# Moving the first weight sums of an MLP behind a different residual addition, at the edge between attention and MLP

## The chip, the cores and the metric

The kernel runs on one core of one Trainium2 chip. The metric is the device time of the whole program in microseconds (us). It is quoted as a median over runs. Where two kernels are compared, the ratio is the mean time of one kernel's fast runs over the mean time of the other's fast runs of the same rounds on the same chip, with a 95% interval. It is therefore not quite the ratio of the medians that stand beside it.

Engines carry the names of the profile: PE is TensorE's matmul unit, DVE is VectorE, ACT is ScalarE, POOL is GpSimd, and SPq is the queue of SyncE, which issues most DMAs. "L560" is line 560 of the kernel. The edits of the experiments shift later lines by up to 18: L640 of the kernel before is L642 or L644 in some runs, L729 is L731, L828 is up to L846.

## The reference

One transformer layer on x of 2048 x 1024 in bf16: linear attention with 32 heads of 32, then a gated MLP with 3584 hidden columns. Each stands behind a layer norm and is added to its input.

```python
def attention(x, wqkv, wo):                 # x: 2048 x 1024, already normalised
    q, k, v = heads(x @ wqkv)               # 32 heads of 32
    phi = lambda t: jnp.where(t > 0, t + 1, jnp.exp(t)) + 1e-6
    pq, pk = phi(q), phi(k)
    kv, z = pk^T @ v, sum(pk)               # per head
    num, den = pq @ kv, pq @ z + 1e-6
    return merge(num / den) @ wo

def mlp(x, W_gate, W_up, W_down):           # x already normalised
    return (relu(x @ W_gate) * (x @ W_up)) @ W_down

h  = x + attention(layernorm(x), wqkv, wo)
h2 = h + mlp(layernorm(h), W_gate, W_up, W_down)
```

## The kernel before

Everything is fused in one program. The large products are computed with a seven-product scheme instead of eight (as Strassen's). A block of four outputs, called a quad here, is computed by the products m1 to m7. These need sums of the left blocks (of the normalised x, `hn`) and sums of the right blocks (of the weights), and VectorE makes both. In the profile, the PSUM tile `Aq` holds m1, then m6, m7 and m4 on top of it, `Dq` holds m2, and `Eq` m5 and then m3. ScalarE copies some of these tiles to SBUF between the products (L154); the copies are called snapshots here.

The change touches one stretch, about 205 to 290 us: the **edge** between attention and the MLP. Rows come in tiles of 128, tile 0 to 15 in the order of work. The first eight tiles give the first half, on which the first MLP quads ("early quads") can start while attention still works on the second half. For each tile the attention stages are these:

- `nd` makes numerators and denominators (PE), then the reciprocal (ACT) and the division (DVE).
- `oT` is a transpose by DMA.
- `wo_h` is the product with wo (PE) and the x addition in two halves (DVE). The addition also frees the PSUM bank that the product stood in. Mean and norm (DVE, ACT) follow.
- `hn_T` is the DMA transpose of the normalised tile, four steps after `nd`; `wo_h` comes two steps after `nd`. For tiles 4 to 7 (and 12 to 15 of the second half), four left sums follow on DVE.

```python
    def left_sums(T, S, cols, eng):                                      # for tiles 4 to 7 of a half
        ...
        eng.tensor_tensor(out=s1, in0=a21, in1=a22, op=ALU.add)          # L117
        eng.tensor_tensor(out=s2, in0=s1, in1=a11, op=ALU.subtract)      # L118
        eng.tensor_tensor(out=a21.bitcast(FP16), in0=a11, in1=a21, op=ALU.subtract)
        eng.tensor_tensor(out=s4, in0=a12, in1=s2, op=ALU.subtract)      # L120

    def phi_end(dst, e):
        nc.scalar.activation(out=e, in_=dst, func=ACT.Exp, bias=negb[:, 0:1], scale=1.0)   # L216
        nc.vector.tensor_scalar(out=e, in0=e, scalar1=1.0, scalar2=PHI_EPS, op0=ALU.min, op1=ALU.add)
        nc.vector.tensor_tensor(out=dst, in0=dst, in1=e, op=ALU.max)                       # L218

        def wo_h(borrow):                                                # of attn_stages(t)
            ...
            for j in range(2):
                ...                                                      # a PSUM bank, ps
                for c in range(KC):
                    nc.tensor.matmul(ps[:], lhsT=st["oT"][:, c, :], rhs=wo_sb[...], ...)   # L557
                with tc.high_priority():
                    added[t] = nc.vector.scalar_tensor_tensor(           # L560, the x addition
                        out=h_sb[...], in0=ps[:], scalar=1.0, in1=h_sb[...],
                        op0=ALU.mult, op1=ALU.add, accum_out=tot[:, j:j + 1])

    def weight_sums(w_sb, fi, nm):                                       # four per weight and quad
        ...
        steps = [first,                                                  # L636
            lambda: tt(out=t[0][:, 1], in0=b[1][1], in1=t[0][:, 0], op=ALU.subtract),   # L640
            lambda: tt(out=t[0][:, 2], in0=b[1][1], in1=b[0][1], op=ALU.subtract),      # L641
            lambda: tt(out=t[0][:, 3], in0=b[1][0], in1=t[0][:, 1], op=ALU.subtract)]   # L642

    # the first early quad begins without its sums; they come later:
    for step in range(QSTEPS + 2, ready):
        if step == QSTEPS + 2:
            flow.pop(0)()
        attn_step(step)
    with tc.issue_after(added[order[STS - 1]].ins):                      # L779, STS = 8
        late_sums.pop()()                                                # 4 gate and 4 up sums
```

A scheduler orders the instructions of each engine in this part. `issue_after` adds one constraint to it: what stands inside is issued behind the instruction named. `added[t]` is overwritten by the second half, so `added[order[7]]` is the last x addition of tile 7.

Of the kernel before, what the change touches and what calls it, by code (L numbers as in the profile page):

```python
# [31 lines left out]
def block_kernel(ctx: ExitStack, tc: tile.TileContext, x, wqkv, wo, wg, wu, wd, out, H: int):  # L32
    nc = tc.nc
# [10 lines left out]
    NW = 512  # L44
# [176 lines left out]
    order = [(i * HS + s * SW) // P + tt for s in range(NS) for i in range(2) for tt in range(NT)]  # L221
# [289 lines left out]
    held, added, squared = [], {}, {}  # L511

    def attn_stages(t):

        i, r = divmod(t * P, HS)
        s, r = divmod(r, SW)
        st = {}

        def nd():
            o_sb = bwork.tile([P, D], BF16, tag="o_sb", name="o_sb")  # L520
            st["o"] = o_sb
            held.append(o_sb)
            ov = o_sb[:].rearrange("p (k h e) -> p k h e", k=KC, h=HPC)
            for c0, n in pieces:
                ps = ndpool.tile([P, NW], FP32, tag="ab", name="nd")
                for c in range(c0, c0 + n):
                    nc.tensor.matmul(ps[:, (c - c0) * NDW:(c - c0 + 1) * NDW], lhsT=pqT[:, c, t * P:(t + 1) * P],
                                     rhs=kvz[:, c, :], start=True, stop=True)
                ndv = ps[:, 0:n * NDW].rearrange("p (k w) -> p k w", w=NDW)
                den = bsmall.tile([P, GPB, HPC], FP32, tag="den", name="den")  # L530
                nc.scalar.activation(out=den[:, 0:n], in_=ndv[:, :, P:NDW], func=ACT.Ln, bias=deps[:], scale=1.0)
                rd = bsmall.tile([P, GPB, HPC], FP32, tag="rd", name="rd")
                nc.scalar.activation(out=rd[:, 0:n], in_=den[:, 0:n], func=ACT.Exp, scale=-1.0)  # L533
                nc.vector.tensor_tensor(  # L534
                    out=ov[:, c0:c0 + n], in0=ndv[:, :, 0:P].rearrange("p k (h e) -> p k h e", h=HPC),
                    in1=rd[:, 0:n, :].unsqueeze(3).to_broadcast([P, n, HPC, Dh]), op=ALU.mult)

        def oT():
            oT = bwork.tile([P, D], BF16, tag="oT", bufs=XB, name="oT")
            st["oT"] = oT[:].rearrange("p (c t) -> p c t", c=KC)  # L540
            nc.sync.dma_start_transpose(out=st["oT"], in_=st["o"][:])

        def x_in():
            x_sb = bwork.tile([P, D], BF16, tag="x_res", bufs=XB, name="x_res")
            nc.sync.dma_start(out=x_sb[:], in_=xf[t * P:(t + 1) * P, :])
            st["x"] = x_sb

        def wo_h(borrow):
            h_sb = st["x"]
            tot = bsmall.tile([P, 2], FP32, tag="tot", name="tot")  # L550
            for j in range(2):
                if borrow:
                    ps = pspool.tile([P, NW], FP32, tag="E", bufs=2, name="attn")
                else:
                    ps = abpool.tile([P, NW], FP32, tag="ab", name="attn")
                for c in range(KC):
                    nc.tensor.matmul(ps[:], lhsT=st["oT"][:, c, :], rhs=wo_sb[:, c, j * NW:(j + 1) * NW],  # L557
                                     start=(c == 0), stop=(c == KC - 1))
                with tc.high_priority():
                    added[t] = nc.vector.scalar_tensor_tensor(out=h_sb[:, j * NW:(j + 1) * NW], in0=ps[:], scalar=1.0,  # L560
                                                   in1=h_sb[:, j * NW:(j + 1) * NW], op0=ALU.mult, op1=ALU.add,
                                                   accum_out=tot[:, j:j + 1])
            nc.sync.dma_start(out=h_dram[i][s][:, r // P, :], in_=h_sb[:])
            st["hn"] = bwork.tile([P, D], BF16, tag="hn", bufs=HB, name="hn")

            sm = bsmall.tile([P, 6], FP32, tag="sm", name="sm")
            nmean, var, lnv, rstd, nmr = (sm[:, i:i + 1] for i in range(5))
            nc.vector.tensor_scalar(out=nmean, in0=tot[:, 0:1], scalar1=tot[:, 1:2], scalar2=-1.0 / D,
                                    op0=ALU.add, op1=ALU.mult)
            squared[t] = nc.scalar.activation(out=st["hn"][:], in_=h_sb[:], func=ACT.Square, bias=nmean, scale=1.0, accum_out=var)  # L570
            nc.scalar.activation(out=lnv, in_=var, func=ACT.Ln, bias=LN_EPS, scale=1.0 / D)
            nc.scalar.activation(out=rstd, in_=lnv, func=ACT.Exp, scale=-0.5)
            nc.scalar.activation(out=nmr, in_=nmean, func=ACT.Identity, scale=rstd)
            nc.scalar.activation(out=st["hn"][:], in_=h_sb[:], func=ACT.Identity, bias=nmr, scale=rstd)

        def hn_T():
            nc.sync.dma_start_transpose(out=hnT[s][i][:, :, r:r + P], in_=st["hn"][:])

        return nd, oT, x_in, wo_h, hn_T

    LAG = (0, 1, 1, 2, 4)
    STS = ST // NS
# [4 lines left out]
    def attn_step(step):  # L587
        for k in range(len(LAG)):
            n = step - LAG[k]
            if n in begin_at:  # L590
                n = begin_at.index(n)
                if k == 3:
                    stages[n][k](QSTEPS <= step < STS + LAG[-1])
                else:
                    stages[n][k]()
                if k == len(LAG) - 1 and n % STS >= NT:
                    left_sums(hnT[n // STS], hns[n // STS], slice(n % NT * P, (n % NT + 1) * P), nc.vector)
# [177 lines left out]
    for step in range(QSTEPS + 2, ready):  # L775
        if step == QSTEPS + 2:
            flow.pop(0)()
        attn_step(step)
    with tc.issue_after(added[order[STS - 1]].ins):  # L779
        late_sums.pop()()  # L780
    steps = QSTEPS + STS + LAG[-1] - ready
    for n in range(steps):
# [19 lines left out]
    def acc(tag):  # L802
        return accs.tile([P, 2 * NW], FP32, tag=tag, bufs=2 if tag == "A" else 1, name="acc" + tag)
# [119 lines left out]
    for r, (wt, f, fi, toks) in enumerate(runs):  # L923
        w = [ops() for _, ops in now]
        later = []
        for n, s in enumerate(toks):
# [51 lines left out]
            if k == nwin - 3:  # L978
                for x in range(2):
                    t = wpools[1].tile([P, KC * 2 * GP * P], BF16, tag=("wg", "wu")[x], name="wd")  # L980
# [16 lines left out]
    for n in range(2):  # L997
        t = fpool.tile([P, 4 * D], BF16, tag="wraw", bufs=2, name="xd")
# [244 lines left out]
    for n in range(1, len(OUTER)):  # L1243
# [73 lines left out]
        else:  # L1317
            pss = []
            for p in range(4):
                ps = acc(("A", "A", "XY"[(n + 1) % 2], "XY"[n % 2])[p])  # L1320
# [24 lines left out]
@with_exitstack  # L1345
def kernel(
    ctx: ExitStack,
    tc: tile.TileContext,
    A_x: bass.AP,
    A_wqkv: bass.AP,  # L1350
    A_wo: bass.AP,
    B_x: bass.AP,
    B_W_gate: bass.AP,
    B_W_up: bass.AP,
    B_W_down: bass.AP,
    out: bass.AP,
):
    block_kernel(tc, A_x, A_wqkv, A_wo, B_W_gate, B_W_up, B_W_down, out, H=32)
# [30 lines left out]
```

## Time and profile before

Three runs gave a median of 738.58 us (737.89 to 739.36).

| stretch before | value | read from |
|---|---|---|
| span of the profiled run | 737.3 us | head of the page |
| PE busy | 724.7 us (98%) | busy time |
| DVE busy in 210 to 220 us | 9.89 of 10 us | windows |
| PE busy in 210 to 220 us | 8.19 of 10 us | windows |
| PE's recorded waits in 203 to 292 us | 2.0 us | waits |
| first matmul of the main quads | 287.84 us | PE's timeline |

The page of the kernel before gives busy time, share of the span and number of instructions by engine. Further down it gives the shares of the chain that ended last:

```profile
PE 724.7 (98%) x4020; PEld 382.1 (52%) x4020; DVE 563.8 (76%) x992; ACT 322.4 (44%) x580; POOL 5.6 (1%) x44
...
PE 82%; DVE 8%; DMA 5%; ACT 4%; issue 1%; SPq 0%; DVEq 0%; POOL 0%; ACTq 0%
```

As a whole the kernel is bound by TensorE. The edge is not. The windows view of the kernel before has the columns stretch, length, busy time and count of PE, PEld, DVE, ACT and POOL, the granted TensorE clock, the DMA share and GB/s:

```profile
210.00:220.00 10.00, 8.19 (x49) 4.02 (x48) 9.89 (x30) 8.55 (x28) 0.00 (x0) 1.00 0.69 129
220.00:230.00 10.00, 9.90 (x53) 4.62 (x51) 8.66 (x23) 7.47 (x22) 0.00 (x0) 1.00 0.96 204
```

In the first of these stretches DVE is full and PE is not. The Trainium skill (Perfetto Trace Analysis, section "Optimization Strategy") says that the most contended engine can change from one regime of a kernel to the next, and that one should look for the gaps of the engine within the regime and for the instruction that ends each. PE's waits in 203 to 292 us of the kernel before are these (who waited for whom: total us, times, longest us):

```profile
PE attn L557 <- DVE x_res L560: 1.3, 1, 1.3
PE nd L527 <- DVE o_sb L534: 0.5, 1, 0.5
PE attn L557 <- DVE o_sb L534: 0.2, 1, 0.2
```

In PE's timeline of the kernel before (start us, length us, engine, line, operation, out<-in, form, count, and in brackets the idle time before and who ended it) the largest is the wo product of tile 9, which waits for tile 8's addition to free a bank:

```profile
207.78 3.61 PE L557 MATMUL attn<-wo_mem,oT 128*128 128x512 bf16 x16
212.73 0.59 PE L557 MATMUL attn<-wo_mem,oT 128*128 128x512 bf16 x2 [1.34 <-DVE x_res L560]
...
219.20 1.03 PE L729 MATMUL Aq<-hs,tg 128*128 128x512 f16 x4
```

DVE's timeline of the kernel before shows what stood ahead of that addition (same columns). The five lines at L636 to L642 are sums of the first quad's weights, `tg` of the gate and `tu` of the up weight. L217 is phi's min and add, L560 the addition. The lines left out are left sums:

```profile
208.63 0.42 DVE L636 TENSOR_TENSOR tg<-wg 128x512 f16<-128x512 bf16 x1
208.97 0.42 DVE L641 TENSOR_TENSOR tg<-wg 128x512 f16<-128x512 bf16 x1
...
209.64 0.42 DVE L640 TENSOR_TENSOR tg<-wg,tg 128x512 f16<-128x512 bf16 x1
...
210.98 0.42 DVE L642 TENSOR_TENSOR tg<-wg,tg 128x512 f16<-128x512 bf16 x1
211.32 0.42 DVE L636 TENSOR_TENSOR tu<-wu 128x512 f16<-128x512 bf16 x1
211.65 0.42 DVE L217 TENSOR_SCALAR e<-e 128x1024 bf16<-128x1024 bf16 x1
211.99 0.68 DVE L560 SCALAR_TENSOR_TENSOR x_res<-attn,x_res 128x512 bf16<-128x512 f32 x1
```

The min/add at L217 needs the exp of ScalarE. ScalarE's timeline of the kernel before has it at:

```profile
209.94 1.14 ACT L216 ACTIVATE e<-pq_mem,negb 128x1024 bf16<-128x1024 bf16 x1
```

Before the change the exp is not what the addition waits for. It ends at 211.08, and VectorE is still at its sums until 211.65.

### The profile page before, as it was taken

What the parts mean: (1) busy time and instruction counts of PE and PEld (TensorE: products, weight loads), DVE (VectorE), ACT (ScalarE), POOL (GpSimd) and SP (SyncE); (2) the same over time, 40 slices, a digit from 0 to 9 for tenths busy, and PEclk for the clock granted to TensorE, in tenths of its full rate; (3) what the DMA queues carried; (4) which work ended last, traced back from release to release, by engine and by line L of the source; (5) the groups of instructions that cost most, each with busy time, mean ns of one, the idle gap of its engine ahead of it and who ended that gap; (6) DMA issues with size and microseconds to landing.
All of it is one profiled execution on the core that took longest, in us unless ns stands there. A gap on an engine that the chain in (4) does not pass through costs nothing.

```text
span 737.3 us, 10605 instructions
## 1 busy us (share of the span) xinstructions
PE 724.7 (98%) x4020; PEld 382.1 (52%) x4020; DVE 563.8 (76%) x992; ACT 322.4 (44%) x580; POOL 5.6 (1%) x44
## 2 busy tenths in 40 slices
PE   7999999999999999999999999999999999999997
PEld 3444555444444444444444444444444468888666
DVE  6997644677788777688768787887786379996797
ACT  4876553778887654444344444443444120000000
POOL 1000000000000000000000000000000000000000
PEclk9999999999999999999999999999999999999999
DMA  9765002079977526175638358575483499987822
GB/s 315 159 151 159 1 1 85 31 159 222 221 172 179 128 73 207 43 207 136 196 103 243 114 187 272 185 218 195 158 284 116 140 396 335 333 288 296 295 81 78
DMA packets 146594, 132.02 MB, mean 179 GB/s; under 512 B 50928, under 2 KB 128112, under 8 KB 146544
## 3 DMA queue, kind: packets, MB, share of 16 engines
q1 hardware_dynamic: 135536, 123.30, 55.8%
q10 hardware_dynamic: 11008, 8.06, 3.4%
q8 instruction: 31, 0.51, 0.3%
q14 instruction: 19, 0.16, 0.1%
HBM read 79.95 MB, written 39.85 MB: 162 GB/s over the span
## 4 chain that ended last, share of the span: by engine, by line
PE 82%; DVE 8%; DMA 5%; ACT 4%; issue 1%; SPq 0%; DVEq 0%; POOL 0%; ACTq 0%
PE accA L828 22%; PE accY L828 8%; PE accX L828 8%; PE accA L1160 8%; PE attn L557 5%; PE Aq L314 3%; PE accA L989 3%; PE accX L1160 3%; PE Aq L454 3%; PE accY L1160 2%; PE Aq L729 2%; PE Eq L314 2%; PE accY L989 2%; PE accX L989 2%; PE Eq L454 1%; PE Eq L729 1%
## 5 line engine op out<-in xcount | busy, mean ns | idle before, releaser
L838 ACT ACTIVATE gu<-gu 128x512 bf16<-128x512 bf16 x72 | 45.4, 630 | 131.2 <-DVE gu L837 131.2
L833 ACT COPY snap<-accA 128x1024 f32<-128x1024 f32 x72 | 72.5, 1008 | 36.5 <-PE accA L828 36.4
L557 PE MATMUL attn<-wo_mem,oT 128*128 128x512 bf16 x256 | 58.7, 379 | 2.7 <-DVE x_res L560 1.3
L828 PEld LDWEIGHTS <-tu 128*128 128x128 f16 x384 | 37.6, 98 | 45.3
L828 PEld LDWEIGHTS <-tg 128*128 128x128 f16 x384 | 37.6, 98 | 45.3
L837 DVE TENSOR_TENSOR gu<-accY,snap 128x1024 bf16<-128x1024 f32 x36 | 43.9, 1219 | 10.0 <-ACT snap L833 10.0
L828 PE MATMUL accA<-hn,tg 128*128 128x512 f16 (+1 forms) x192 | 49.3, 379 | 0.0
L828 PE MATMUL accA<-hn,tu 128*128 128x512 f16 (+1 forms) x192 | 49.3, 379 | 0.0
L837 DVE TENSOR_TENSOR gu<-accX,snap 128x1024 bf16<-128x1024 f32 x36 | 43.9, 1219 | 6.4 <-PE accX L828 3.7
L154 ACT COPY u<-Aq 128x512 f32<-128x512 f32 x54 | 31.3, 582 | 36.0 <-PE Aq L314 19.3
L1160 PEld LDWEIGHTS <-x 128*128 128x128 f16 (+1 forms) x448 | 43.9, 98 | 5.5
L828 PEld LDWEIGHTS <-wu 128*128 128x128 bf16 x288 | 28.2, 98 | 34.0
L828 PEld LDWEIGHTS <-wg 128*128 128x128 bf16 x288 | 28.2, 98 | 34.0
L557 PEld LDWEIGHTS <-oT 128*128 128x128 bf16 x256 | 24.7, 98 | 33.0 <-issue 4.9
L841 DVE TENSOR_TENSOR hq<-gu 128x512 bf16<-128x512 bf16 x48 | 20.3, 423 | 14.3 <-ACT gu L838 14.2
L314 PEld LDWEIGHTS <-xT 128*128 128x128 bf16 (+1 forms) x192 | 18.6, 98 | 23.7 <-issue 2.3
L534 DVE TENSOR_TENSOR o_sb<-nd,rd 128x384 bf16<-128x384 f32 (+1 forms) x48 | 23.2, 508 | 8.8 <-ACT rd L533 6.6
L1160 PEld LDWEIGHTS <-xs 128*128 128x128 f16 x280 | 27.4, 98 | 3.2
L560 DVE SCALAR_TENSOR_TENSOR x_res<-attn,x_res 128x512 bf16<-128x512 f32 x32 | 22.0, 686 | 8.4 <-PE attn L557 8.2
L989 PEld LDWEIGHTS <-x 128*128 128x128 bf16 (+1 forms) x168 | 16.4, 98 | 19.6
L1166 DVE TENSOR_TENSOR snap<-accA,u 128x1024 f32<-128x1024 f32 x16 | 19.5, 1220 | 8.3 <-PE accA L1160 8.1
L828 PE MATMUL accA<-hs,tg 128*128 128x512 f16 x96 | 24.6, 379 | 0.0
(234 smaller groups left out, 1406.1 us busy)
## 6 DMA issues: line engine op xcount, KB each, us to landing
x<-x_dram SPq DMA_DIRECT2D x17, 896.0 KB, 8.3
x_dram<-hq SPq DMA_DIRECT2D x28, 512.0 KB, 3.2
wg<-in_B_W_gate_dram SPq DMA_DIRECT2D x14, 512.0 KB, 5.2
wu<-in_B_W_up_dram SPq DMA_DIRECT2D x14, 512.0 KB, 7.3
wraw<-in_B_W_down_dram SPq DMA_DIRECT2D x14, 512.0 KB, 5.0
x_dram<-hq SPq DMA_DIRECT2D x28, 256.0 KB, 2.6
t_dram<-wt SPq DMA_DIRECT2D x28, 256.0 KB, 2.2
xd<-x_dram SPq DMA_DIRECT2D x6, 896.0 KB, 7.2
```

What stands on the lines that cost most here:

```text
L154: copies[nm, v] = nc.scalar.copy(out=snaps[nm, v], in_=bank[v][:])
L314: nc.tensor.matmul(ps[:], lhsT=left[m - 1][:, kc, r + v * P:r + (v + 1) * P], rhs=right[m - 1][:, kc, :], start=(start and kc == 0), stop= ...
L454: nc.tensor.matmul(ps[:], lhsT=rq[m - 1][:, kc, (c + v) * P:(c + v + 1) * P], rhs=left[m - 1][:, kc, :], start=(start and kc == 0), stop=( ...
L534: nc.vector.tensor_tensor(out=ov[:, c0:c0 + n], in0=ndv[:, :, 0:P].rearrange("p k (h e) -> p k h e", h=HPC), in1=rd[:, 0:n, :].unsqueeze(3 ...
L557: nc.tensor.matmul(ps[:], lhsT=st["oT"][:, c, :], rhs=wo_sb[:, c, j * NW:(j + 1) * NW], start=(c == 0), stop=(c == KC - 1))
L729: nc.tensor.matmul(ps[:], lhsT=w(v, m)[:, kc, :], rhs=left[m - 1][:, kc, :], start=(start and kc == 0), stop=(kc == KH - 1), skip_group_ch ...
L828: nc.tensor.matmul(ps[:, v, :], lhsT=w[v][n - 1][:, kc, :], rhs=left[n - 1][:, kc, :], start=(t is not None and kc == 0), stop=(kc == KH - ...
L833: nc.scalar.copy(out=st[nm][:], in_=halves(st["A"]))
L837: add(out=g[:], in0=halves(st[nm]), in1=st[base][:], op=ALU.add)
L838: nc.scalar.activation(out=g[:, 0, :], in_=g[:, 0, :], func=ACT.Relu)
L989: nc.tensor.matmul(ps[:, t * NW:(t + 1) * NW], lhsT=x_tile(n, s, kh)[:, f, (t0 + t) * P:(t0 + t + 1) * P], rhs=w_tile(n, kh)[:, f, :], sta ...
L1160: nc.tensor.matmul(pv[:, tt, :], lhsT=left(m)[:, f, tt * P:(tt + 1) * P], rhs=right(m)[:, f, :], start=(t is not None and f == 0 and tt % ...
```

## The change

Its intent is to take the first quad's weight sums out of the way of tile 8's first x addition. The constraint names tile 8's first addition instead of tile 7's last.

```diff
-                    added[t] = nc.vector.scalar_tensor_tensor(out=h_sb[:, j * NW:(j + 1) * NW], ...
+                    added[t, j] = nc.vector.scalar_tensor_tensor(out=h_sb[:, j * NW:(j + 1) * NW], ...
@@
-    with tc.issue_after(added[order[STS - 1]].ins):
+    with tc.issue_after(added[order[STS], 0].ins):
         late_sums.pop()()
```

The number of instructions is the same. A comparison of the two built programs' instruction orders (it has no times) shows that all five sums leave the place in front of tile 8's first addition. One sum stands ahead of tile 9's first addition, where another stood before. Seven follow the left sums made after that, where two stood. PE's order follows: in the first quad four gate matmuls of m5 instead of two come first and m5 of the up weight comes earlier, and in the second quad seven m6 matmuls now stand ahead of tile 12's wo matmuls.

More of the change, by code (lines that the diff above doesn't have):

```diff
@@ L559, in wo_h @@
                 with tc.high_priority():
-                    added[t] = nc.vector.scalar_tensor_tensor(out=h_sb[:, j * NW:(j + 1) * NW], in0=ps[:], scalar=1.0,
+                    added[t, j] = nc.vector.scalar_tensor_tensor(out=h_sb[:, j * NW:(j + 1) * NW], in0=ps[:], scalar=1.0,
                                                    in1=h_sb[:, j * NW:(j + 1) * NW], op0=ALU.mult, op1=ALU.add,
```

## The prediction

> **What bounds the kernel.** TensorE. The page gives it 724.7 us busy of a 737.3 us span at full clock; the chain of waits is 82% PE. The change touches only the edge between attention and the early MLP quads, about 205 to 290 us. The stretch view (10 us slices, 200 to 290) shows PE idle there for about 2.3 us, 1.8 of it in 210 to 220: no reordering here can win more (0.3%).
>
> **The gap.** PE waits twice: 1.34 us at 212.73 (wo matmuls of tile 9) for the first x addition of tile 8 (211.99, 0.68 us), which frees their PSUM bank, then 0.48 us at 213.80 (numerators) for the division behind it. In VectorE's timeline five weight sums stand ahead of that addition, 208.63 to 211.65, 0.335 us apart: 1.67 us. The Trainium skill (PSUM — Partial Sum Buffer, "Engine vs sequencer instructions") says that VectorE's and ScalarE's queues are strict FIFO; the trace agrees: the addition's matmuls had ended near 209.6.
>
> **What the change does.** Nothing is added or removed. The comparison of instruction orders shows all five sums leaving that place; one sum of the first quad stays ahead of tile 9's first addition (where another stood), seven follow tile 9's left sums, where two stood. PE's order follows: four instead of two m5 gate matmuls first, m5 of the up weight earlier, and in the second quad seven m6 matmuls ahead of tile 12's wo matmuls.
>
> **Worth on the critical path.**
> - Not 1.67 us. Before the addition stands phi's min/add on VectorE (211.65), which needs ScalarE's exp, 209.94 to 211.08, in an unchanged ScalarE order. So the min/add starts near 211.13, the addition near 211.47, PE near 212.2: gain 0.52 us. The 0.48 us gap moves along and stays.
> - Given back: tile 9's left sums end near 219.2, the first quad's m6 gate sum near 219.6, while PE, after Dq x4 and Eq x4 (8 x 0.216 us), is ready at 219.1: a new stall of 0.4 to 0.5 us. The up weight's first sum ends near 220.65, PE ready at 220.5: another 0.1 to 0.2.
> - VectorE's backlog is then 1.1 us larger, until its idle time at 227 to 230 absorbs it.
> - Weight matmuls ahead of later wo groups may close the gaps at 228.8, 239.2 and 249.0 (0.09, 0.10, 0.24 us): up to 0.4 gained. m7 directly before m4 may cost 0.1 to 0.3 waiting for ScalarE's snapshots.
>
> Sum: -0.5 +0.6 -0.4 +0.15, about -0.2 us; from 290 us on nothing changes. These are estimates from the trace's starts and durations.
>
> **Prediction:** 738.4 us, 80% range 737.3 to 739.6 (runs of before: 737.9 to 739.4). Faster by over 2%: 0.005; within 2%: 0.985; slower by over 2%: 0.01.
>
> **What the profile should show.**
> 1. Tile 8's first addition starts 0.5 us earlier (not 1.7), directly behind the min/add that waits for the exp.
> 2. PE's 1.34 us wait shrinks to about 0.8; the 0.5 us one for the division stays.
> 3. A new PE wait on a weight sum, 0.3 to 0.7 us near 219.5.
> 4. PE's idle time from 200 to 290 within 1 us of 2.3; the first main quad (287.84 before) starts within 1 us of that.
> 5. Equal instruction counts; PE busy equal within 0.5 us.
>
> **What would make it wrong.** A late buffer release or DMA transpose (the queue's order of oT and hn changes), stalling 1 to 3 us in the second or third quad; a larger sum stall because tile 9's transposed tile lands later; or, the other way, hidden sums and closed gaps, a gain of 1 to 2 us.

One name in it is wrong. The "left sums of tile 9" and "tile 9's transposed tile" are those of tile 7: in the first half left sums are made for tiles 4 to 7 only, and they come two steps later than the wo product. The times given there are of the right instructions.

## The result

The changed kernel took 739.2 us (median of 6 runs, 739.13 to 739.61). The kernel before took 738.94 us beside it (6 runs, 737.88 to 740.4). The ratio is 1.0005, with a 95% interval of 0.9992 to 1.0018: the same time. The changed kernel was correct, and its profiled run ended at full clock, with a span of 737.3 us, equal to the one before.

The page of the changed kernel:

```profile
PE 722.0 (98%) x3967; PEld 381.7 (52%) x4020; DVE 563.8 (76%) x992; ACT 321.6 (44%) x580; POOL 5.6 (1%) x44
...
PE 84%; DVE 6%; DMA 5%; ACT 4%; issue 1%; SPq 0%; DVEq 0%; POOL 0%; ACTq 0%
```

PE's 722.0 is not a gain of 2.7 us. The trace lacks 53 matmul records (3967 against 4020), while the weight loads, which match the matmuls one for one before, are 4020 in both. A second trace of the changed kernel (`e6_after_again`), with all 4020 records, has 725.5 us. DVE's busy time is equal to the digit. The windows of the changed kernel:

```profile
210.00:220.00 10.00, 8.26 (x48) 3.83 (x47) 9.02 (x26) 9.07 (x33) 0.00 (x0) 1.00 0.78 151
220.00:230.00 10.00, 9.92 (x50) 4.37 (x50) 9.46 (x26) 6.23 (x17) 0.00 (x0) 1.00 0.70 179
```

VectorE's work went from the first stretch (9.89 to 9.02 us) to the second (8.66 to 9.46 us). The sum of both is 18.55 us before and 18.48 us after. PE gained nothing that could be seen: 18.09 and 18.18 us, the second with records missing.

PE's waits of the changed kernel in 203 to 292 us:

```profile
PE attn L557 <- DVE x_res L560: 0.8, 1, 0.8
PE nd L527 <- DVE o_sb L534: 0.5, 1, 0.5
PE Aq L729 <- DVE tg L640: 0.4, 1, 0.4
PE attn L557 <- DVE o_sb L534: 0.4, 1, 0.4
```

This is the whole result in small. The list adds up to 2.1 us, against 2.0 us before. The half microsecond that left the first line has come back in the third and fourth. PE's timeline of the changed kernel shows where:

```profile
207.44 3.61 PE L557 MATMUL attn<-wo_mem,oT 128*128 128x512 bf16 x15
211.86 0.59 PE L557 MATMUL attn<-wo_mem,oT 128*128 128x512 bf16 x2 [0.81 <-DVE x_res L560]
...
219.53 1.04 PE L729 MATMUL Aq<-hs,tg 128*128 128x512 f16 x4 [0.45 <-DVE tg L640]
...
249.84 3.61 PE L557 MATMUL attn<-wo_mem,oT 128*128 128x512 bf16 x15 [0.40 <-DVE o_sb L534]
```

In DVE's timeline of the changed kernel the five sums are gone from the place ahead of the addition. Only 0.53 us of their 1.67 us are won, because the min/add now stands idle for 0.94 us, waiting for the exp. At 219 the sums are late in turn, directly behind the last left sums:

```profile
210.78 0.43 DVE L217 TENSOR_SCALAR e<-e 128x1024 bf16<-128x1024 bf16 x1 [0.94 <-ACT e L216]
211.12 0.69 DVE L560 SCALAR_TENSOR_TENSOR x_res<-attn,x_res 128x512 bf16<-128x512 f32 x1
...
218.72 0.42 DVE L120 TENSOR_TENSOR hs<-hn,hs 128x512 f16<-128x512 bf16 x1
219.06 0.42 DVE L640 TENSOR_TENSOR tg<-wg,tg 128x512 f16<-128x512 bf16 x1
```

The exp itself, in ScalarE's timeline of the changed kernel, starts 0.34 us earlier, as much as PE's wo product of tile 8 (207.44 against 207.78):

```profile
209.60 1.14 ACT L216 ACTIVATE e<-pq_mem,negb 128x1024 bf16<-128x1024 bf16 x1
```

The addition therefore starts 1.52 us after the exp's start, where before it started 2.05 us after it.

The chain of work that ended last says the same in another way (start us, length us, what). In this stretch of the kernel before it ran through the weight sums:

```profile
209.06 0.34 DVE tg L641
...
211.32 0.42 DVE tu L636
211.74 0.34 DVE e L217
212.07 0.07 DVE x_res L560
```

In the changed kernel it no longer does. It runs through ScalarE's exp and norm, then a DMA transpose of tile 7, its left sums, and only then a weight sum:

```profile
209.71 1.04 ACT e L216
...
211.28 1.17 ACT hn L574
...
212.86 4.70 DMA hn<-hn
...
217.58 0.43 DVE hs L117
...
219.14 0.35 DVE tg L640
```

One chain was shortened. Another, nearly as long, took its place.

### The profile page after: what moved, and what is told of

It reads as the page before. It is cut to its first block, busy times and chain, and to the rows that moved or that the text cites. A ratio compares the mean times of both kernels' runs of the same rounds, so it can differ in the third digit from the quotient of the medians.

```text
span 737.3 us, 10550 instructions
## 1 busy us (share of the span) xinstructions
PE 722.0 (98%) x3967; PEld 381.7 (52%) x4020; DVE 563.8 (76%) x992; ACT 321.6 (44%) x580; POOL 5.6 (1%) x44
## 4 chain that ended last, share of the span: by engine, by line
PE 84%; DVE 6%; DMA 5%; ACT 4%; issue 1%; SPq 0%; DVEq 0%; POOL 0%; ACTq 0%
PE accA L828 22%; PE accX L828 8%; PE accY L828 8%; PE accA L1160 8%; PE attn L557 6%; PE Aq L314 3%; PE Aq L729 3%; PE accA L989 3%; PE accX L1160 3%; PE Aq L454 3%; PE accY L1160 2%; PE Eq L314 2%; PE accY L989 2%; PE accX L989 2%; PE Eq L729 2%
## 5 line engine op out<-in xcount | busy, mean ns | idle before, releaser
L828 PEld LDWEIGHTS <-tu 128*128 128x128 f16 x384 | 37.6, 98 | 45.3
L828 PEld LDWEIGHTS <-tg 128*128 128x128 f16 x384 | 37.6, 98 | 45.3
L828 PE MATMUL accA<-hn,tu 128*128 128x512 f16 (+1 forms) x192 | 49.3, 379 | 0.0
L828 PE MATMUL accA<-hn,tg 128*128 128x512 f16 (+1 forms) x192 | 49.3, 379 | 0.0
L828 PEld LDWEIGHTS <-wu 128*128 128x128 bf16 x288 | 28.2, 98 | 34.0
L828 PEld LDWEIGHTS <-wg 128*128 128x128 bf16 x288 | 28.2, 98 | 34.0
L828 PE MATMUL accA<-hs,tg 128*128 128x512 f16 x96 | 24.6, 379 | 0.0
```

Of the source, the lines that this page charges most:

```text
L828: nc.tensor.matmul(ps[:, v, :], lhsT=w[v][n - 1][:, kc, :], rhs=left[n - 1][:, kc, :], start=(t is not None and kc == 0), stop=(kc == KH - ...
```

## The experiments

**The theory of two chains** is that of the prediction, extended by what the traces showed. The edge is paced by VectorE and ScalarE together. Taking the sums away wins only what is left above the exp, and the sums come back later, in front of PE, because VectorE's total work is unchanged. **The rival of PE's order**: the gain was won, and PE's new order (seven m6 matmuls ahead of tile 12's wo) gave it back. **The inert rival**: nothing at the edge matters, because TensorE's volume sets its end. The expectations quoted below were written before each run and use the names and the knowledge of that moment.

The runs were sent in three jobs. The kernel before ran in each: median 739.0 us in the first (11 runs, 738.48 to 741.2), 739.05 in the second (11 runs), 739.38 in the third (11 runs). Most main differences are below 1 us, so a ruler better than the total time was needed. Two facts made one.

- From the first main quad on, the length hardly differs. The span minus the start of that quad is 449.45 to 449.55 us in eleven of the twelve traces (449.1 in `e4_sums_on_pool`).
- The launches differ before the edge. PE reaches the first early quad anywhere between 204.6 and 207.3 us. The Trainium skill (TensorE: Matmul & The Clock Gate, section "What's actually happening") says that the clock is throttled by default, that activity releases it, and that an idle window of about 3.4 us brings it back to half. The traces agree in the main. Near the start PE waits once for VectorE (`tp<-ident,xn`, at 9 to 10 us). This wait was 3.71, 3.02 and 3.24 us in `e5_before_again`, `e6_after_again` and `e8_both_phi_second`; the granted clock then fell to 0.50 until 14 to 15 us, and PE reached the edge at 206.5 to 207.3. In the other nine traces it was 1.63 to 2.63 us, the clock in 10 to 20 us was 1.00, and PE reached the edge at 204.6 to 205.5.

The ruler used below is therefore the time **from the start of the last exp (L216) to the first main-quad matmul (L828)**. Why it starts at the exp and not at PE is told at the repeats. The expectations still use the length from tile 8's first wo matmul to the main quads. It came out at 80.06 and 79.51 us (before, e5), 80.38 and 79.42 (after, e6), 79.66 (e1), 79.76 (e2), 79.21 and 78.51 (e3, e9), 79.63 (e8), 81.66 (e7) and 86.12 (e4). So e1 and e3 lie inside what the theory of two chains expected, and e5, e6, e7 and e8 outside.

| trace | last exp | tile 8's first addition | first main matmul | exp to main | ratio of times [95%] |
|---|---|---|---|---|---|
| before | 209.94 | 211.99 | 287.84 | 77.90 | |
| e5_before_again | 211.06 | 213.11 | 289.00 | 77.94 | 1.0007 [0.9991, 1.0023] |
| after | 209.60 | 211.12 | 287.82 | 78.22 | 1.0005 [0.9992, 1.0018] |
| e6_after_again | 210.06 | 211.58 | 288.09 | 78.03 | 0.9998 [0.9982, 1.0013] |
| e1_two_early | 208.73 | 210.25 | 286.95 | 78.22 | 0.9986 [0.9973, 0.9999] |
| e2_phi_late | 209.13 | 209.29 | 286.75 | 77.62 | 0.9991 [0.9975, 1.0006] |
| e3_both | 209.99 | 210.69 | 287.04 | 77.05 | 0.9982 [0.9969, 0.9995] |
| e9_both_again | 208.62 | 209.33 | 285.71 | 77.09 | 0.9986 [0.9968, 1.0003] |
| e8_both_phi_second | 211.42 | 212.12 | 288.89 | 77.47 | 0.9981 [0.9966, 0.9996] |
| e7_m6_behind | 209.45 | 210.96 | 288.94 | 79.49 | 1.0016 [1.0002, 1.0031] |
| e4_sums_on_pool | 209.92 | 216.67 | 293.88 | 83.96 | 1.0072 [1.0057, 1.0087] |
| e10_rd_first | 205.94 (moved) | 210.06 | 290.38 | not comparable, see e10 | 1.0035 [1.0016, 1.0054] |

All outputs were correct.

### Two sums early, so that PE does not wait for them at 219 (e1)

The sums that the first m6 and m5 products need are put back where VectorE has 0.94 us of idle time; the rest stay behind tile 8's addition. The second quad's sums are held behind tile 9's second addition, so that the scheduler cannot fill the freed place with them.

```diff
+            if f == 1:
+                with tc.issue_after(added[order[STS + 1], 1].ins):
+                    sums()
+            elif f:
                 sums()
@@
+    gate, up = all_sums(early[0], 0)
+    with tc.issue_after(added[order[STS - 1], 1].ins):
+        for f in gate[0][:2]:
+            f()
     with tc.issue_after(added[order[STS], 0].ins):
-        late_sums.pop()()
+        for f in gate[0][2:] + up[0]:
+            f()
```

> After the change, with two of the eight sums (the gate's first and second) put back ahead of tile 8's first x addition, and the second quad's sums held behind tile 9's additions so that they cannot fill the place. Edge length = from tile 8's first wo matmul to the first main-quad matmul: before 80.06 us, after 80.38. Queue theory (VectorE's order decides, and 0.94 us of it was idle behind the exp): the addition stays as early as after the change (about 3.7 us behind the start of tile 8's wo matmuls; before it was 4.2), the 0.45 us wait for the second gate sum goes, edge length 79.5 to 79.9. Rival (the edge's idle time is not what sets the time, later waits take it up): wait gone but edge length 80.0 to 80.4. Time of the whole kernel within 0.3% of before either way.

Measured: 738.57 us (738.23 to 738.72, 5 runs). The addition again starts 1.52 us after the exp, and PE's wait for a weight sum is gone. In its place stands, in PE's timeline of this kernel, a wait for tile 7's left sum:

```profile
217.71 0.59 PE L729 MATMUL Eq<-hs,tg 128*128 128x512 f16 x2 [0.51 <-DVE hs L117]
```

In DVE's timeline of the same kernel, that left sum waits for the DMA transpose:

```profile
217.23 0.43 DVE L117 TENSOR_TENSOR hs<-hn 128x512 f16<-128x512 bf16 x1 [0.62 <-DMA hn<-hn]
```

It follows that the weight sums were not alone at 219. The chain exp, norm, transpose, left sum stands right behind them. With the sums out of the way PE waits for the transpose about as long as it had waited for the sum (0.51 against 0.45 us), and exp to main stays 78.22 us. That length is not this wait's alone: the scheduler also changed PE's order further on (tile 12's wo matmuls start at 237.39 us, ahead of m2 and m6).

### Phi's min/add and max behind the addition (e2)

This takes away what caps the gain: the addition need not wait for the exp if phi's last two VectorE steps stand behind it.

```diff
-        nc.vector.tensor_scalar(out=e, in0=e, scalar1=1.0, scalar2=PHI_EPS, op0=ALU.min, op1=ALU.add)
-        nc.vector.tensor_tensor(out=dst, in0=dst, in1=e, op=ALU.max)
+        a = nc.vector.tensor_scalar(...)                       # unchanged
+        phi_end.last = a, nc.vector.tensor_tensor(...)         # unchanged
@@ tile 7's left sums, held where they were
+                    ctx7 = tc.issue_after(added[order[STS + 1], 1].ins) if n == STS - 1 else ExitStack()
@@ behind the late sums
+    for i in phi_end.last:                                     # an order on VectorE, no data
+        tc.add_manual_dep(i.ins, added[order[STS], 0].ins.name, ...)
```

> After the change, with the last phi's min/add and max on VectorE put behind tile 8's first x addition (tile 7's left sums held behind tile 9's additions). If the exp is what capped the gain: the addition starts 2.3 to 2.6 us behind the start of tile 8's wo matmuls instead of 3.7, tile 9's wo matmuls no longer wait (0.81 us after the change), the wait for the division stays near 0.45. VectorE cannot pass the exp by more than the one addition, so edge length falls by 0.3 to 0.5 only, to about 80.0 us; the 0.45 us wait for the second gate sum stays. Rival (the addition is bound by something else): start stays at 3.5 to 3.7.

Measured: 738.57 us (737.71 to 740.56, 6 runs). The addition starts 0.16 us after the exp's start, 2.30 us after the wo matmuls', as expected, and PE's wait for it is gone. This settles what capped the gain of the change: it was the exp. The expectation missed on the next wait. The division's wait was to stay at about 0.45 us; it is 0.85 us, in PE's timeline of this kernel:

```profile
211.45 0.33 PE L527 MATMUL nd<-kvz,pq_mem 128*128 128x132 bf16 x3 [0.85 <-DVE o_sb L534]
```

Two waits that had stood one behind the other have become one. Of the 1.3 us of both in the changed kernel (0.81 and 0.48), 0.4 us is saved. The wait for a weight sum, 0.45 us, stays.

### Both edits (e3, and again as e9)

> Both of these edits together. Queue theory: the addition 2.9 to 3.2 us behind the start of the wo matmuls, tile 9's wo matmuls wait under 0.2, no wait for a weight sum, edge length 79.1 to 79.6; the kernel about 0.7 to 1.0 us faster than after (0.1%), not to be resolved by times alone. Rival of a downstream that takes it up: 80.0 or more.

Measured: 738.37 us (737.69 to 738.5, 5 runs). Exp to main is 77.05 us, 0.9 us less than before and 1.1 us less than after (means of the two traces each, 77.92 and 78.13). PE has no wait for the x addition or for a weight sum; the division's is 0.87 us. The windows view of this kernel shows PE's busy time in this stretch at 9.12 us, against 8.26 after, with VectorE as full as before the change:

```profile
210.00:220.00 10.00, 9.12 (x53) 4.38 (x52) 9.89 (x30) 9.36 (x31) 0.00 (x0) 1.00 0.63 141
```

Neither edit alone gave this: against the changed kernel's mean of 78.13 us, the first came out 0.1 us longer and the second 0.5 us shorter. The first leaves the cap, and the second leaves the wait for the sums. The same program was run again, to see whether the smallest edge of the series repeats.

> e3_both once more, the version that beat both kernels. Measured from the start of the last phi's exp on ScalarE to the first main-quad matmul, the two traces of before gave 77.90 and 77.94 us, those of after 78.22 and 78.03, e3_both 77.05. If that clock is the right one, this trace gives 76.9 to 77.3 whatever the start of the launch did; time ratio to before 0.998 to 0.9995.

Measured: 737.96 us (737.0 to 738.3, 6 runs), exp to main 77.09 us, inside the range expected. PE's only listed wait is 0.4 us near 248; the 0.87 us wait of e3 is gone. The result repeats within 0.04 us. It refutes the inert rival: an order of work that differs only at the edge moves the end of the edge by 0.9 us.

By the times this version beats the kernel before by 0.18 and 0.14% (the first interval leaves out 1, the second just does not). These shares are hardly the edge's alone. Of the kernel before, 4 of 11 runs in the first job and 5 of 11 in the third have a mean clock of 0.998 or less, as in the traces with the slow start; of e3 and e9 none has. Among runs at 0.999 or above the means differ by 0.6 and 0.3 us. The interval of e1 leaves out 1 too, though its ruler shows no gain. Against the changed kernel, which did not run in these jobs, only the ruler speaks.

### Phi behind the second addition (e8)

As e3, with one word changed: phi's two steps behind the second half of tile 8's addition, to let the division through earlier.

```diff
-        tc.add_manual_dep(i.ins, added[order[STS], 0].ins.name, ...)
+        tc.add_manual_dep(i.ins, added[order[STS], 1].ins.name, ...)
```

> As e3_both, with the last phi behind the second addition of tile 8 instead of the first, so that the division that frees the numerators' bank comes directly behind the first addition. Queue theory: PE's wait for that division falls from 0.87 to 0.35 to 0.6 us, edge length 78.6 to 79.1, the shortest of all; the whole kernel at or below e3_both's 0.9982 of before. Rival (VectorE is full there, so what one wait loses the next one gains): edge length stays at 79.1 to 79.5.

Measured: 737.96 us (737.65 to 740.19, 6 runs), exp to main 77.47 us, so 0.4 us more than e3. The division's wait stays at 0.87 us. The scheduler let two more sums slide in front of the second addition. The place that phi left on VectorE did not stay empty. The times cannot tell e8 from e3 (0.9981 and 0.9982 of before).

### The same two programs once more (e5, e6)

A comment line was added and nothing else, to see how far one trace can be trusted.

> The kernel before once more, unchanged, for a second trace: how far do the edge's numbers repeat? If the waits of the edge belong to the order of the queues, the two waits (1.34 and 0.48 us) repeat within 0.15 us and the edge length (80.06) within 0.2. If they are chance, they differ by as much as before and after do.

> The kernel after the change once more, unchanged. Repeats: waits 0.81, 0.48 and 0.45 us within 0.15, edge length 80.38 within 0.2, so longer than the second trace of before by 0.1 to 0.5. If it comes out shorter than before's second trace, the 0.3 us that the first pair of traces shows is not the change's. Times: ratio to before between 0.999 and 1.001.

Measured: the kernel before took 740.31 us (738.41 to 740.7, 6 runs), the changed one 739.14 us (738.18 to 740.52, 6 runs). The expectation that the waits repeat within 0.15 us failed for the largest one. In the second trace of the kernel before the 1.34 us wait is 0.75 us, and in that of the changed kernel the 0.81 us wait is gone. The other waits repeat (0.48, 0.41 and 0.40 us in the changed kernel). What differs is when the exp comes, seen from PE. It starts 1.39 to 1.57 us after tile 8's first wo matmul in these two traces and in e1 and e9, and 2.14 to 2.17 us after it in the others (e10 aside). A PE that is late against the exp waits less; to reach the edge late is not enough (e8 did, and waits 0.87 us). Measured from PE the edge is elastic: from tile 8's first wo matmul to the main quads it took 80.06 and 79.51 us in the two traces of before. Measured from the exp it took 77.90 and 77.94 us. That is why the table uses the exp. No edit but e10's moved it: in all eleven other traces it starts 4.78 or 4.79 us after tile 5's first left sum (L117, 205.16 us in the kernel before), which waits for a DMA transpose.

By this ruler the changed kernel is 0.2 us longer than before (78.22 and 78.03), which the times are too coarse to confirm or to deny. By the measure of the expectation it came out shorter (79.42 against 79.51 us), and the expectation said that the 0.3 us of the first pair is then not the change's. The ruler was chosen after these traces; e9, sent after it was chosen, is its test.

### PE's new order undone (e7)

The rival of PE's order is tested by holding the second quad's m6, m5 and second m2 behind tile 12's wo matmuls, nearly PE's order of before, while VectorE keeps the new one.

```diff
+                if fc == 1 and (m in (5, 6) or m == 2 and v):
+                    m6_mm.append(i)
@@
+    for i in m6_mm:
+        tc.add_manual_dep(i.ins, wo_mm[order[12]].ins.name, ...)
```

> After the change, with one of its side effects on TensorE undone: the second quad's m6 matmuls (and what follows them, m2 of the up weight and m5) again behind tile 12's wo matmuls; VectorE's order of the first quad's sums stays as the change has it. If that side effect made the wait at 249 us grow (0.24 to 0.40): tile 12's additions come 1.3 to 1.6 us earlier, that wait falls back to 0.15 to 0.3, and the wait at 239 us that the change closed (0.10) returns; edge length 80.1 to 80.5. If the growth at 249 us has another cause it stays at 0.35 to 0.45.

Measured: 740.43 us (740.03 to 741.67, 6 runs), exp to main 79.49 us, 1.3 us longer than in the changed kernel. The wait at 249 did shrink from 0.40 to 0.24 us as expected. The large miss is at 240, in PE's timeline of this kernel:

```profile
240.39 3.61 PE L557 MATMUL attn<-wo_mem,oT 128*128 128x512 bf16 x16 [1.46 <-DVE o_sb L534]
```

Tile 12's wo matmuls start only 0.4 us earlier than in the changed kernel, not the 1.3 to 1.6 us expected, because they need a bank that a division frees, and that division is late in both. The traces show where it comes from. In the changed kernel and in e7, five m4 matmuls of the first quad stand ahead of tile 11's wo matmuls, which stood ahead of m4 before. PE's timelines of the kernel before and of the changed kernel:

```profile
228.85 1.89 PE L557 MATMUL attn<-wo_mem,oT 128*128 128x512 bf16 x8
...
230.23 3.61 PE L557 MATMUL attn<-wo_mem,oT 128*128 128x512 bf16 x15
```

Tile 11's second addition follows at 232.79 and 233.99 us. Its mean (L568) is at 233.51 us before and at 235.21 after; the norm's first step on ScalarE (L570) at 234.07 and 235.45; the reciprocal, behind it on ScalarE, at 238.42 and 239.87; the division at 238.67 and 240.12. The Trainium skill (PSUM — Partial Sum Buffer, section "Engine vs sequencer instructions") says that ScalarE's and VectorE's queues are strict FIFO, and the traces agree: the reciprocal kept its place behind a norm that came 1.4 us later and was late by as much (1.45 us). In the changed kernel seven m6 matmuls fill the 1.5 us. So the rival falls as it was put: the m6 matmuls ahead of tile 12 are not the cost; without them the change would have lost 0.2%. The other part of PE's new order, m4 ahead of tile 11, made most of the hole that they fill: the second addition is 1.2 us later of the mean's 1.7. No run undoes it, so what it costs alone is not shown; e3 and e9 have it too, and are 0.9 us shorter than before.

### The first quad's sums on GpSimd (e4)

This takes the eight sums off VectorE altogether.

```diff
-            st["w"] = run_sums(early[f // GP], f % GP)
+            st["w"] = run_sums(early[f // GP], f % GP, nc.gpsimd if f < 1 else None)
@@
-    with tc.issue_after(added[order[STS], 0].ins):
-        late_sums.pop()()
+    late_sums.pop()()
```

(Tile 7's left sums and the second quad's sums are held as in e1 and e2.)

> After the change, with the first quad's eight sums on GpSimd instead of VectorE (the second quad's held behind tile 9's additions). It takes 2.7 us off VectorE's queue between 205 and 222. Queue theory: the addition stays at 3.7 us (bound by the exp), no wait for a gate sum provided GpSimd does the first three sums within 12 us, edge length 79.2 to 79.8. Against: if GpSimd needs over 3 us a sum, or VectorE's own instructions grow by 10% or more beside it, waits of 1 us or more for the sums appear and the edge is longer than 80.4.

Measured: 744.81 us (744.43 to 745.33, 5 runs), the slowest of all. The second possibility named in the expectation came true in the main: VectorE's left sums grew and the edge is longer, but PE waited for the addition and not for a sum. While GpSimd made its sums, as in this line of POOL's timeline of the kernel,

```profile
209.63 1.33 POOL L638 TENSOR_TENSOR tu<-wu 128x512 f16<-128x512 bf16 x1
```

VectorE's left sums, with two inputs in SBUF, took about three times as long, and its operations with one SBUF input did not (as the addition at 206.08, beside GpSimd's first sum at 206.11). DVE's timeline of the same kernel:

```profile
206.08 0.68 DVE L560 SCALAR_TENSOR_TENSOR x_res<-attn,x_res 128x512 bf16<-128x512 f32 x1
...
208.58 1.38 DVE L119 TENSOR_TENSOR hn<-hn,hn 128x512 f16<-128x512 bf16 x1
...
216.67 0.68 DVE L560 SCALAR_TENSOR_TENSOR x_res<-attn,x_res 128x512 bf16<-128x512 f32 x1
```

The left sum of L119 takes 0.42 us in the kernel before. The Trainium skill (SBUF — State Buffer, section "Who interferes with whom") says just this: a VectorE instruction with two SBUF inputs contends with a GpSimd instruction that reads SBUF, and one with at most one SBUF input does not (outside its faster two-port modes). The trace agrees: each of the seven left sums ended 0.27 to 0.29 us after the end of the GpSimd sum that it overlapped. Tile 8's addition was thereby held up by 4.7 us (216.67 against 211.99, with the exp at 209.92 and 209.94), and PE, in its timeline of this kernel, by as much:

```profile
217.41 1.01 PE L557 MATMUL attn<-wo_mem,oT 128*128 128x512 bf16 x2 [6.03 <-DVE x_res L560]
```

From within this gap until about 220 us the granted clock in the windows view was 0.50.

### The reciprocal ahead of tile 7's norm (e10)

As e3, with tile 7's Square (the norm's first step on ScalarE) held behind tile 10's first reciprocal, to shorten the 0.87 us wait that is left.

```diff
+    tc.add_manual_dep(squared[order[STS - 1]].ins, rds[order[STS + 2], 0].ins.name, ...)
```

> e3_both with the reciprocals of tile 10's denominators put ahead of tile 7's square on ScalarE, so that the division behind tile 8's first addition need not wait for the exp. If ScalarE's order is what bounds PE's last wait there (0.87 us for the division): that wait falls under 0.4 us, the first main quad starts 0.3 to 0.8 us earlier than in e9_both_again measured from the same arrival. If VectorE is simply full, the waits reappear behind it and nothing is gained.

Measured: 741.68 us (740.28 to 742.95, 6 runs), 0.35% slower than before. The wait fell to 0.53 us only, and not under 0.4 as expected. The edit also moved the exp, to 205.94 us, so the ruler is taken from tile 5's first left sum: 86.28 us to the main quads, against 81.87 in e9 and 82.68 and 82.72 before. The price came through the DMA queue: the transpose of tile 7, issued at 213.25 us in e3, was issued at 215.62 behind another transpose, though its norm ended no later (7.6 us after tile 5's first left sum in both). DVE's timeline of this kernel:

```profile
218.93 0.42 DVE L117 TENSOR_TENSOR hs<-hn 128x512 f16<-128x512 bf16 x1 [1.51 <-DMA hn<-hn]
```

and PE's:

```profile
219.41 1.09 PE L731 MATMUL Eq<-hs,tg 128*128 128x512 f16 x3 [2.49 <-DVE hs L117]
220.29 1.91 PE L731 MATMUL Aq<-hs,tg 128*128 128x512 f16 x4
```

Again the clock dropped behind the gap. The four m6 matmuls took 1.91 us, where the changed kernel needs 1.04 for them, and the windows view of this kernel has 0.50 in its clock column:

```profile
221.00:222.00 1.00, 1.00 (x4) 0.30 (x3) 1.00 (x4) 0.97 (x2) 0.00 (x0) 0.50 1.04 348
```

This shows from the other side what e1 showed: the transpose of tile 7 is close behind, and delaying it costs PE at once.

## Why the prediction was right, point by point

That the time fell into the range says little. The range (737.3 to 739.6 us) is about as wide as the scatter of the kernel before (737.88 to 740.4), and PE was idle for only 2.3 us in the whole stretch. The middle, 738.4, was 0.8 us too low. What counts are the points on the mechanism.

1. *The addition starts 0.5 us earlier, not 1.7, behind a min/add that waits for the exp.* Right: 0.53 us earlier relative to the exp, with 0.94 us of recorded idle before the min/add. e2 showed that the exp is the cap, by taking it away.
2. *The wait of 1.34 us shrinks to about 0.8, the one of 0.5 stays.* Right in the first trace (0.81 and 0.48), but half of this was luck. The first wait depends on when PE arrives, seen from the exp. It was 0.75 us in the second trace of the kernel before, and zero in that of the changed one.
3. *A new wait on a weight sum of 0.3 to 0.7 us near 219.5.* Right: 0.45 us at 219.53, and 0.41 in the second trace. e1 showed that the wait for the sum hides another, of about the same size, for tile 7's transpose. The prediction had this chain only among what could go wrong.
4. *PE's idle time within 1 us of before, the main quads within 1 us.* Right: listed waits of 2.1 against 2.0 us; in the windows view of 200 to 290 us idle time of 2.3 us before and at most 2.6 after (records are missing); main quads at 287.82 against 287.84 us.
5. *Equal counts, PE busy equal within 0.5 us.* DVE and ACT instructions and weight loads are equal in count. PE busy differs by 2.7 us in the first pair of traces, because 53 records are missing. The second pair is complete: 725.4 us before, 725.5 after. Right.

Some terms were mis-sized, without much effect on the total: "-0.4" for closing the gaps at 228.8, 239.2 and 249.0 came to about nothing. The gap at 249 grew from 0.24 to 0.40 us, and at 228.8 PE waited 0.15 and 0.21 us for ScalarE's snapshots instead (gaps between the lines of PE's timeline at 228.95 and 230.02). Those snapshots, "+0.15", took 0.36 us. So the sum was about +0.2 us by the exp's ruler where "about -0.2" was predicted. The difference of 0.4 us is 0.05% of the run. VectorE's larger backlog was absorbed as predicted: an addition of the first quad (`gu<-Eq`, L738) starts at 228.94 us in both traces, in the changed kernel after 0.43 us of idle time. What came late after that, tile 11's mean by 1.7 us, came mostly from the weight matmuls ahead of tile 11's wo matmuls. The prediction had counted such matmuls only as a gain, for the gaps they fill.

What stays open: whether the 0.2 us is real, since the changed kernel's own two traces differ by 0.19 us. Also what the 0.87 us wait left in e3 is worth: e9, the same program, did not have it, and e10, built to shorten it, moved the exp and a transpose as well. And what m4 ahead of tile 11 costs.

## What to carry to other kernels

Before moving work out of an engine's way, look at what the freed instruction waits for next, and at where the moved work lands: a stretch with a full engine only gains if the second chain is shortened too, as here, where neither half of the best edit was worth as much alone and both together took 0.9 us off the edge. A scheduler fills a freed place with whatever is ready, so compare the instruction orders of the built programs, and hold what must not slide in. When the differences are smaller than the scatter of launches, build a ruler inside the trace, from an instruction of the limiting chain to the first one behind which all traces agree, and test it on repeats of the same program.

## What the Trainium skill lacked or had wrong

- TensorE: Matmul & The Clock Gate, section "What's actually happening", puts the fall to half clock at an idle window of about 3.4 us. In e10 one recorded wait of 2.49 us was followed by a granted clock of 0.50 from 220 to 223 us; waits of 1.34 (before) and 1.46 us (e7) were not. Near the start, waits of 3.02 to 3.71 us were followed by a fall and those of 1.63 to 2.63 us were not. Recorded waits shorter than the page's window can thus cost a slow phase of about 3 us, and the length of the wait alone does not decide it.
- SBUF — State Buffer, section "Who interferes with whom", says that whoever issues first holds the shared ports and the other blocks, but gives no size for this pair of instructions. In e4 both ran slower, very unequally: VectorE's left sums of 128x512 went from 0.42 to between 1.05 and 1.38 us, GpSimd's sums from 1.15 to about 1.33 us. The first sum of 1.15 us ran at 206.11, when VectorE had none of its left sums under way.
- Perfetto Trace Analysis, section "Optimization Strategy", tells to find the gap and what ends it. It does not say that a gap's length depends on when the waiting engine arrives: the same program's largest wait was 1.34 us in one trace and 0.75 us in another, while the chain behind it repeated within 0.04 us.
- No page on reading a trace warns that PE's busy time can come out short because records are lost: 53 of 4020 were missing in one trace, which looked like 2.7 us of PE's work.
